# Fp32 state products on tiles of the PE array, weights kept in SBUF, and one string for every engine's order

## The chip, the cores and the metric

The kernel runs on one core of a Trainium2 chip. The metric is the device time of one execution in microseconds (us). Engines are named as the profile names them: PE is TensorE's matmul side and PEld its weight loads, DVE is VectorE, ACT is ScalarE, POOL is GpSimd, SP is the engine that issues all DMA transfers here.

## The reference

Eight batches b, eight heads h, 512 positions, 32 state rows, 64 numbers a head. Attention runs both ways between x and a small state, then the rows (512 of x and 32 of the state per batch) go through a two-layer network with softplus:

```python
scores = scale * np.matmul(x, state.transpose(0, 1, 3, 2))     # 512 x 32 per head
a = softmax(scores);   xread = np.matmul(a, state)
scores2 = scale * np.matmul(state, x.transpose(0, 1, 3, 2))    # 32 x 512 per head
a2 = softmax(scores2); sread = np.matmul(a2, x)
x = concat([xread, sread], axis=2) -> (8 * 544, 512)           # heads side by side
h = x @ w_in                                                   # 512 x 2048, float64 in memory
out = softplus(h) @ w_out                                      # 2048 x 512, float64 in memory
```

## The kernel before, in words

**Splitting.** The two layers run as fp32r matmuls. Each operand is split into a high part (a cast to fp32r, line 90, or line 83 on POOL) and a low part (the rest, line 91), and three products replace one (`PASSES`). The weights come as pairs of 32-bit words; `as_f32` (lines 102 to 116) makes fp32 of them with one ACT operation (line 111) and two of DVE (lines 114, 115).

**The state product.** The read `a @ state @ w_in` is associated the other way: for each batch V = state @ w_in is formed once per head, 256 x 2048 (32 state rows times 8 heads), and the first layer is a @ V (`gemm1`, line 475). So x's read is never formed. V of batches 0 to 3 comes from plain fp32 matmuls with a stationary matrix in which zeros pad each head (`QZ`; `make_v0`, lines 158 and 167, 256 columns each; `make_vf`, lines 200 and 211, 512 columns). Batches 0 and 1 stay in SBUF, 2 and 3 are written to DRAM (`Vd`). For batches 4 to 7 w_in, which was written to DRAM as fp32 (`wsc`), is read again, each head's 64 rows are split (`head`, lines 249 and 250) and multiplied with `StK` (`product`, line 235); the result goes to DRAM as well and is fetched by `fetch_v`. `split_v` makes the high and low part of a piece of 256 columns.

**Attention.** Per batch and half of the heads: scores (batches 0 and 1: plain fp32 with a zero-padded state, line 341; later: split x and split state, line 347), transposed 32 x 32 on DVE (355), maximum, subtraction, exp, sum, product, transposed back (371) and split; the state's side has exp (380), four PE transposes (392), the read of x (405 in plain fp32 for batches 0 and 1, 411 split) and a turn back (439 or 448).

**The layers.** A slot is one column tile of 128 of the hidden layer for one batch: six matmuls at line 475, softplus on ACT (462), the split, twelve matmuls at line 482 into four banks. 128 slots for x's rows and eight wider ones for the state's rows (`gemm1_read`, line 522), 136 softplus in all. Batches 0 and 1 take turns at first.

**Order.** Strings (`START`, `BLOCK`, `LAST`) give the order in which steps are written; the tile scheduler may then move instructions of an engine past one another. `MOVED` lists the operations that go to DVE or POOL instead of the usual engine. Of the eight PSUM banks two hold h, two everything of attention (`aux`) and four the second layer's sums.

Of the kernel before, what the change touches and what calls it, by code (L numbers as in the profile page):

```python
# [39 lines left out]
MOVED = {('R', 1, 0, 0, 0), ('R', 1, 0, 3, 0), ('R', 1, 0, 3, 1), ('R', 1, 1, 0, 0), ('R', 1, 1, 2, 0), ('R', 1, 1, 3, 1), ('R', 1, 2, 1, 0), ('R', 1, 3, 1, 0), ('at', 0, 1), ('at', 2, 1), ('at', 3, 0), ('g', 0, 13), ('g', 0, 5), ('g', 0, 6), ('g', 0, 7), ('g', 0, 8), ('g', 0, 9), ('g', 1, 1), ('g', 1, 10), ('g', 1, 11), ('g', 1, 12), ('g', 1, 14), ('g', 1, 7), ('g', 1, 8), ('g', 1, 9), ('g', 2, 2), ('g', 2, 5), ('g', 2, 6), ('g', 2, 7), ('g', 2, 8), ('g', 3, 6), ('g', 4, 10), ('g', 4, 11), ('g', 4, 7), ('g', 4, 8), ('hi', 'R', 1, 0, 1, 1), ('hi', 'R', 1, 0, 2, 1), ('hi', 'R', 1, 0, 3, 0), ('hi', 'R', 1, 0, 3, 1), ('hi', 'R', 1, 1, 3, 1), ('hi', 'R', 1, 2, 0, 1), ('hi', 'at', 1, 0), ('hi', 'at', 2, 0), ('hi', 'at', 3, 0), ('hi', 'g', 0, 13), ('hi', 'g', 0, 14), ('hi', 'g', 0, 5), ('hi', 'g', 0, 6), ('hi', 'g', 0, 9), ('hi', 'g', 1, 15), ('hi', 'g', 1, 7), ('hi', 'g', 1, 8), ('hi', 'g', 2, 1), ('hi', 'g', 2, 13), ('hi', 'g', 2, 15), ('hi', 'g', 2, 6), ('hi', 'g', 4, 12), ('hi', 'g', 4, 6), ('hi', 'g', 4, 8), ('hi', 'g', 4, 9), ('hi', 'g', 8, 2), ('hi', 'g', 8, 3), ('hi', 'g', 8, 4), ('hi', 'g', 8, 6), ('hi', 'v', 0, 1), ('hi', 'v', 0, 7), ('hi', 'v', 1, 1), ('hi', 'v', 1, 3), ('hi', 'v', 1, 5), ('hi', 'v', 1, 7), ('hi', 'v', 2, 2), ('hi', 'v', 2, 3), ('hi', 'v', 2, 5), ('hi', 'v', 2, 7), ('hi', 'v', 3, 1), ('hi', 'v', 4, 7), ('hi', 'wout', 0), ('hi', 'wout', 13), ('hi', 'wout', 14), ('hi', 'wout', 15), ('hi', 'wout', 7), ('hi', 'xh', 2, 0, 0), ('hi', 'xh', 2, 1, 0), ('hi', 'xs', 2, 0, 0), ('hi', 'xs', 2, 1, 1), ('hi', 'xs', 3, 1, 1), ('sr', 1, 0), ('tmul', 0, 0), ('tmul', 0, 1), ('tmul', 1, 1), ('tmul', 3, 0), ('tmul', 3, 1), ('tsub', 0, 0), ('v', 0, 0), ('v', 0, 3), ('v', 1, 0), ('v', 1, 4), ('v', 1, 5), ('v', 2, 3), ('v', 2, 7), ('v', 3, 0), ('v', 3, 2), ('v', 4, 7), ('v0', 0, 0, 1), ('v0', 0, 2, 2), ('v0', 1, 0, 2), ('v0', 1, 1, 1), ('v0', 1, 1, 2), ('v0', 1, 3, 2), ('vd', 3, 1, 0), ('vd', 3, 1, 1), ('vd', 3, 3, 0), ('ve', 0, 1, 5), ('ve', 0, 2, 1), ('ve', 0, 2, 3), ('ve', 0, 3, 1), ('ve', 0, 3, 7), ('ve', 1, 0, 1), ('ve', 1, 0, 2), ('ve', 1, 0, 3), ('ve', 1, 0, 6), ('ve', 1, 0, 7), ('ve', 1, 1, 0), ('ve', 1, 1, 1), ('ve', 1, 2, 5), ('ve', 1, 3, 4), ('wout', 0), ('wout', 15), ('xh', 2, 1, 0), ('xh', 2, 1, 1), ('xs', 2, 0, 1), ('xs', 2, 1, 0), ('xs', 3, 0, 1)}  # L40
# [5 lines left out]

@with_exitstack
def attention_then_softplus_mlp(ctx: ExitStack, tc, xn, xt, zq, zp, stk, w_in, w_out, out):
    nc = tc.nc
    nc.scalar.preload_act_table_set("natural_log_exp_and_others")  # L50
# [3 lines left out]
    dp = ctx.enter_context(tc.tile_pool(name="dp", bufs=1, space=DRAM))  # L54
    ps = ctx.enter_context(tc.tile_pool(name="ps", bufs=1, space=PSUM))
    uid = [0]

    def sb(tag, shape, dt=F32, bufs=1):
        uid[0] += 1
        return sp.tile(shape, dt, tag=tag, name=f"{tag}_{uid[0]}", bufs=bufs)  # L60

    def bank(tag, bufs):
        uid[0] += 1
        return ps.tile([P, 512], F32, tag=tag, name=f"{tag}_{uid[0]}", bufs=bufs)

    BANKS = {"aux": 2, "h": 2, "acc": 4}
    turn = cycle(("h", "acc", "acc"))
    early = [True]

    def aux():  # L70
        if early[0]:
            tag = next(turn)
            return bank(tag, BANKS[tag])
        return bank("aux", 2)

    ident = cp.tile([P, P], F32, name="ident")
    make_identity(nc, ident)

    def vec(*what):
        return nc.gpsimd if what in MOVED else nc.vector  # L80

    def pool_copy(dst, src):
        nc.gpsimd.tensor_scalar(dst, src, 1.0, 0.0, ALU.mult, ALU.add)  # L83


    def split(hi, lo, src, *what):
        if ("hi",) + what in MOVED:
            pool_copy(hi, src)
        else:
            nc.scalar.copy(hi, src)  # L90
        vec(*what).tensor_tensor(lo, src, f32(hi), ALU.subtract)  # L91

    def load_w(src, tag=None):
        w64 = src.dtype == I64
        tag = tag or ("k4" if w64 else "wt")
        t = sb(tag, src.shape, I64 if w64 else F32, bufs=K4 if tag == "k4" else 2)
        nc.sync.dma_start(t, src)
        return t
# [3 lines left out]


    def as_f32(t, tag="wt"):
        if t.dtype != I64:
            return t
        v = t.bitcast(I32).rearrange("p (n t) -> p n t", t=2)
        lo, hi = v[:, :, 0], v[:, :, 1]
        n = t.shape[1]
        h2 = sb("k2", [P, n], bufs=K2)  # L110
        nc.scalar.activation(h2, f32(hi), AF.Prelu, scale=2.0 ** -112, alpha=-(2.0 ** 32))  # L111
        r = sb(tag, [P, n], bufs=2 if tag == "wt" else 1)
        u = r.bitcast(I32)
        nc.vector.tensor_scalar(u, lo, 29, None, ALU.logical_shift_right)
        nc.vector.scalar_tensor_tensor(u, h2.bitcast(I32), 3, u, ALU.logical_shift_left, ALU.bitwise_or)  # L115
        return r

    wout = {}
    sreadT = cp.tile([P, 2, 4, B * NS], F32R, name="sreadT")
    Z4 = cp.tile([P, 4, P], F32, name="Z4")  # L120
    nc.gpsimd.memset(Z4, 0.0)

    ev = [0]

    def evac(dst, src):  # L130
        ev[0] += 1
        if ev[0] % 2:
            nc.vector.tensor_copy(dst, src)
        else:
            nc.scalar.copy(dst, src)  # L135

    wsc = [dp.tile([DM, 512], F32, tag=f"wsc{c}", name=f"wsc{c}") for c in range(4)]
    Vd = {}
    for c in range(4):
        Vd[0, c] = dp.tile([P, 4, 512], F32, tag=f"vd0_{c}", name=f"vd0_{c}")  # L140
        Vd[1, c] = dp.tile([H, P, 512], F32, tag=f"vd1_{c}", name=f"vd1_{c}")

    VTAGS = {1: ("wout10", "wout11"), 2: ("wout13", "wout14"), 3: ("vf", "vf")}
    QZ = [sb("QZ", [P, 4, P]), sb("wout15", [P, 4, P])]
    Vf, Vhl = {}, {}
    made = {}

    def make_v0():
        for b in range(2):
            Vf[b, 0] = sb("vf", [P, 2, 512], bufs=2)  # L150
        for half in range(2):
            cs = slice(256 * half, 256 * half + 256)
            for q in range(4):
                k = 4 * half + q
                wt = as_f32(first.pop(0), tag=f"wout{4 + k}" if k < 6 else "wt")
# [4 lines left out]
                for b in range(2):  # L160
                    dst, src = Vf[b, 0][r, q // 2, cs], pb[64 * b:64 * b + 64, 0:256]
                    if ("v0", half, q, b) in MOVED:
                        nc.vector.tensor_copy(dst, src)
                    else:
                        nc.scalar.copy(dst, src)
# [137 lines left out]
    def load_z(b):  # L303
# [9 lines left out]
        zin[b] = z  # L313

# [257 lines left out]

# [128 lines left out]
```

## Time and profile before

| | |
|---|---|
| three runs | 713.04, 713.7, 715.2 us; median 713.7 |
| span of the profiled execution | 709.8 us (its own time is not recorded beside it) |
| median less span | 3.9 us |
| PE, ACT, DVE, POOL busy | 96%, 60%, 54%, 24% of the span |
| first matmul of the first layer | at 32.70 us |
| HBM read and written | 56.62 MB, 25.69 MB |

The span runs from the first to the last instruction of the core. A matmul's record reaches from its start to its modelled end, so neighbours overlap: the gap between starts is what one costs in a full stream. A row of a group has the line, the engine, the operation, output and inputs, shapes, the count, then busy us and mean ns of one, then the idle time of the engine ahead of it with what ended that. Plain fp32 matmuls appear as two records each, fp32r ones as one.

### The profile page before, as it was taken

What the parts mean: (1) busy time and instruction counts of PE and PEld (TensorE: products, weight loads), DVE (VectorE), ACT (ScalarE), POOL (GpSimd) and SP (SyncE); (2) the same over time, 40 slices, a digit from 0 to 9 for tenths busy, and PEclk for the clock granted to TensorE, in tenths of its full rate; (3) what the DMA queues carried; (4) which work ended last, traced back from release to release, by engine and by line L of the source; (5) the groups of instructions that cost most, each with busy time, mean ns of one, the idle gap of its engine ahead of it and who ended that gap; (6) DMA issues with size and microseconds to landing.
All of it is one profiled execution on the core that took longest, in us unless ns stands there. A gap on an engine that the chain in (4) does not pass through costs nothing.

```text
span 709.8 us, 8853 instructions
## 1 busy us (share of the span) xinstructions
PE 678.6 (96%) x3012; PEld 534.1 (75%) x3012; DVE 384.2 (54%) x682; ACT 423.5 (60%) x701; POOL 172.9 (24%) x170
## 2 busy tenths in 40 slices
PE   5689899999999999999999999999999999999997
PEld 2455566888877778877788887888788888878886
DVE  4587547834696885595646633664376323432101
ACT  3699999935476575788658633863486334333222
POOL 1230102565333366111200070007000500100220
PEclk9999999999999999999999999999999999999999
DMA  8777767221244455364333321221012023412001
GB/s 273 267 261 259 262 212 242 98 60 40 80 141 148 149 166 186 116 193 155 120 104 108 101 59 31 97 83 30 30 53 67 22 70 90 149 30 60 1 0 59
DMA packets 42059, 82.87 MB, mean 117 GB/s; under 512 B 6176, under 2 KB 13088, under 8 KB 42016
## 3 DMA queue, kind: packets, MB, share of 16 engines
q1 hardware_dynamic: 42016, 82.33, 36.2%
q8 instruction: 23, 0.38, 0.2%
q14 instruction: 20, 0.16, 0.1%
HBM read 56.62 MB, written 25.69 MB: 116 GB/s over the span
## 4 chain that ended last, share of the span: by engine, by line
PE 75%; ACT 9%; DVE 7%; DMA 5%; issue 3%; SPq 1%; POOL 1%; DVEq 0%; ACTq 0%; POOLq 0%
PE acc L482 44%; PE h L475 20%; PE h L522 4%; DMA k<-in_w_in_dram 2%; PE aux L235 2%; ACT t L462 2%; PE aux L411 1%; DMA vf<-vd 1%; DVE glo L91 1%; PE aux L347 1%; DMA QZ<-in_zq_dram 1%; ACT k L111 1%; ACT ghi L90 1%; DMA vd<-ve 1%; PE aux L200 1%
## 5 line engine op out<-in xcount | busy, mean ns | idle before, releaser
L482 PE MATMUL acc<-wout,ghi 128*128 128x512 f32 x1088 | 344.2, 396 | 0.3 <-ACT o L135 0.3
L482 PEld LDWEIGHTS acc<-wout,ghi 128*128 128x128 f32 x1088 | 204.1, 189 | 47.9 <-issue 3.6
L482 PE MATMUL acc<-wout,glo 128*128 128x512 f32 x544 | 214.5, 394 | 0.0
L475 PE MATMUL h<-aT,vhl 128*128 128x512 f32 x768 | 200.6, 398 | 5.1 <-ACT t L462 3.7
L475 PEld LDWEIGHTS h<-aT,vhl 128*128 128x128 f32 x768 | 141.3, 188 | 43.9 <-ACT t L462 11.0
L91 DVE TENSOR_TENSOR glo<-t,ghi 128x512 fp32r<-128x512 f32 x100 | 71.9, 719 | 123.2 <-ACT ghi L90 65.0
L462 ACT ACTIVATE t<-h 128x512 f32<-128x512 f32 x136 | 81.1, 599 | 93.2 <-PE h L475 46.3
L482 PEld LDWEIGHTS acc<-wout,glo 128*128 128x128 f32 x544 | 102.4, 188 | 23.2 <-issue 1.2
L90 ACT CAST ghi<-t 128x512 fp32r<-128x512 f32 x104 | 64.6, 621 | 81.4 <-PE acc L482 80.6
L91 DVE TENSOR_TENSOR vhl<-vf,vhl 128x512 fp32r<-128x512 f32 x62 | 45.0, 726 | 89.2 <-ACT vhl L90 79.8
L83 POOL TENSOR_SCALAR ghi<-t 128x512 fp32r<-128x512 f32 x32 | 22.8, 712 | 175.3 <-PE acc L482 147.7
L91 POOL TENSOR_TENSOR glo<-t,ghi 128x512 fp32r<-128x512 f32 x36 | 49.0, 1362 | 46.0 <-ACT ghi L90 45.0
L90 ACT CAST vhl<-vf 128x512 fp32r<-128x512 f32 x59 | 36.5, 618 | 30.4 <-PE h L522 16.8
L368 POOL TENSOR_TENSOR T<-T,sm 128x512 f32<-128x512 f32 x13 | 13.7, 1052 | 136.7 <-DVE sm L367 136.2
L462 ACT ACT_TABLE_LOAD x30 | 38.5, 1283 | 3.9 <-PE h L475 3.4
L522 PEld LDWEIGHTS h<-sreadT,vhl 128*128 128x128 f32 x192 | 23.4, 191 | 4.4 <-ACT t L462 4.4
L522 PE MATMUL h<-sreadT,vhl 128*128 128x256 f32 x192 | 25.1, 287 | 1.1 <-ACT t L462 1.0
L352 DVE TENSOR_TENSOR k<-aux,k 64x512 f32<-64x512 f32 x24 | 16.4, 683 | 16.7 <-ACT k L351 16.4
L111 ACT ACTIVATE k<-k 128x512 f32<-128x512 f32 (+1 forms) x32 | 20.1, 642 | 8.6 <-DMA k<-in_w_in_dram 7.8
L115 DVE SCALAR_TENSOR_TENSOR wt<-k,wt 128x512 int32<-128x512 int32 (+1 forms) x26 | 20.0, 777 | 6.2 <-ACT k L111 5.8
L250 DVE TENSOR_TENSOR R<-wt,R 64x512 fp32r<-64x512 f32 x24 | 18.4, 768 | 6.9 <-ACT R L249 3.8
L235 PE MATMUL aux<-R,StK 128*128 128x512 f32 x64 | 20.0, 401 | 0.1
(162 smaller groups left out, 692.0 us busy)
## 6 DMA issues: line engine op xcount, KB each, us to landing
vd<-ve SPq DMA_DIRECT2D x44, 256.0 KB, 2.8
xT<-in_xt_dram SPq DMA_DIRECT2D x16, 512.0 KB, 4.1
x<-in_xn_dram SPq DMA_DIRECT2D x16, 512.0 KB, 3.9
k<-in_w_out_dram SPq DMA_DIRECT2D x16, 512.0 KB, 4.7
vf<-vd SPq DMA_DIRECT2D x64, 128.0 KB, 2.6
k<-in_w_in_dram SPq DMA_DIRECT2D x12, 512.0 KB, 5.4
out_dram<-o SPq DMA_DIRECT2D x24, 256.0 KB, 2.2
wt<-wsc SPq DMA_DIRECT2D x16, 256.0 KB, 2.9
```

The source lines that it names most:

```text
L83: nc.gpsimd.tensor_scalar(dst, src, 1.0, 0.0, ALU.mult, ALU.add)
L90: nc.scalar.copy(hi, src)
L91: vec(*what).tensor_tensor(lo, src, f32(hi), ALU.subtract)
L111: nc.scalar.activation(h2, f32(hi), AF.Prelu, scale=2.0 ** -112, alpha=-(2.0 ** 32))
L115: nc.vector.scalar_tensor_tensor(u, h2.bitcast(I32), 3, u, ALU.logical_shift_left, ALU.bitwise_or)
L235: nc.tensor.matmul(pb, StK[i][:, h, :], r, start=(i == 0), stop=(i == 1))
L250: vec("R", *what, o).tensor_tensor(r[z], wf[a], f32(r[a]), ALU.subtract)
L352: nc.vector.tensor_tensor(sc[64 * j:64 * j + 64], pb[0:64], s2, ALU.add)
L462: nc.scalar.activation(t, h, AF.Softplus)
L475: nc.tensor.matmul(h, Vhl[b, ft // 2][:, vi, g, cs], aT[b][:, ai, g], start=(n == 0), stop=(n == 5))
L482: nc.tensor.matmul(acc[c], g[gi][:, c0:c0 + P], wout[ft][:, wi], start=(ft == first and i == 0), stop=(ft == last and i == 2))
L522: nc.tensor.matmul(h[:, 256 * i:256 * i + 256], Whl[u, i][:, wi, kt, :], sreadT[:, si, kt, :], start=(n == 0), stop=(n == 11))
```

## The change

1. **Tiles.** `heads` multiplies, for one batch, the eight heads' states with w_in (or with x transposed): head 2q+e has its 64 numbers in partitions 64e to 64e+63, and its 32 state rows become output partitions 32q to 32q+31 of bank e. Each is one plain fp32 matmul of 64 x 32 with `tile_position=(64e, 32q)`. V for all batches (`v_product`, 33 calls: 31 of 512 columns, two of 256) and the scores of all batches (8 calls) are made in this way. The read of x (`s_read`, 16 calls) uses 128 x 32 tiles in plain fp32, four heads side by side, 64 columns each, 16 matmuls a call; the turn back (`s_back`) two 128 x 64 tiles.
2. **No scratch.** w_in is converted once and stays in SBUF as fp32 (`W`, 32 KB a partition); `wsc`, `Vd`, their writes and reads, `QZ`, `StK` and `z`'s split go. V is split straight out of the two banks, once per piece.
3. **Rooms.** SBUF tiles come from 27 rooms of 2 KB and 26 of 4 KB a partition (and five small ones), all eight PSUM banks from one list; a room is given out again in the order in which rooms were freed.
4. **Order.** A string of 1577 letters (`PLAN`) says which step is written next, `ENG` which engine takes each cast or element-wise step; `keep_in_program_order` holds each engine to that order, DMA issues on SP included.

The layers' matmuls, their shapes, the turns of batches 0 and 1 and the order of the slots are the same.

```diff
+class Ordered:
+    class Engine:
+        def __getattr__(self, name):
+            f = getattr(self.engine, name)
+            return lambda *a, **k: self.tc.keep_in_program_order(f(*a, **k))
...
+class Rooms:
+    def take(self, shape=None, dt=F32, uses=1):
+        tag = self.free.popleft()
...
+        t = self.pool.tile(shape or self.shape, dt, tag=tag, name=f"{tag}_{self.made}", bufs=1)
...
+    r2 = Rooms(sp, "s", N2, [P, 512])
+    r4 = Rooms(sp, "d", N4, [P, 2, 512])
+    banks = Rooms(ps, "b", 8, [P, 512])
...
+    ST = cp.tile([P, B, 4, 2 * NS], F32, name="ST")
+    W = cp.tile([P, 4, DFF], F32, name="W")
...
+    def heads(out_e, b, rhs):
+        for q in range(4):
+            for e in range(2):
+                r = slice(64 * e, 64 * e + 64)
+                nc.tensor.matmul(out_e[e][32 * q:32 * q + 32], ST[r, b, q, 32 * e:32 * e + 32], rhs(q)[r], start=True, stop=True,
+                                 tile_position=(64 * e, 32 * q))
+    def v_product():
+        for b, i in VLIST:
+            c0, c1 = units(b)[i]
+            t = Vb[b, i] = [banks.take(uses=2) for _ in range(2)]
+            heads([a[:, 0:c1 - c0] for a in t], b, lambda q: W[:, q, c0:c1])
...
+    def v_hi():
+                cast(t[0].t, Vb[b, i][e][:, 0:c1 - c0], engine())
+    def v_lo():
+                nc.vector.tensor_tensor(t[1].t, Vb[b, i][e][:, 0:c1 - c0], f32(t[0].t), ALU.subtract)
...
+    def scores():
+            heads(t, b, lambda q: xT[b, q // 2][:, q % 2])
...
+    def s_read():
+            for c in range(4):
+                for q in range(4):
+                    h = 2 * q + e
+                    nc.tensor.matmul(pr[k][32 * q:32 * q + 32, 0:D], a2T[k][:, P * c + 32 * q:P * c + 32 * q + 32],
+                                     x[b, h // 4][:, c, D * (h % 4):D * (h % 4) + D], start=(c == 0), stop=(c == 3),
+                                     tile_position=(0, 32 * q))
...
-    wsc = [dp.tile([DM, 512], F32, tag=f"wsc{c}", name=f"wsc{c}") for c in range(4)]
-                nc.tensor.matmul(pb, QZ[0][:, q, :], wf, start=True, stop=True)
-            nc.tensor.matmul(pb, StK[i][:, h, :], r, start=(i == 0), stop=(i == 1))
-        nc.sync.dma_start(Vd[1, c][h], ve)
...
+    run = {k: f() for k, f in steps.items()}
+    for k in PLAN:
+        now[0] = k
+        count[k] = count.get(k, 0) + 1
+        next(run[k])
```

PE around the first two first-layer matmuls, before: `aux`, `h` and `acc` are banks, `a2T` the state's weights turned, `vhl` split V. The rows at line 475 are the two.

```order
L405 MATMUL h_309<-x_206,a2T_307 128x256 x4
L341 MATMUL aux_316<-xT_257,Z_73 128x512 x2
L439 MATMUL h_344<-ident,sr_114 128x128 x4
L475 MATMUL h_357<-aT_113,vhl_297 128x512 x6
L475 MATMUL h_466<-aT_113,vhl_297 128x512 x6
L158 MATMUL acc_334<-wt_330,QZ_87 128x256
```

And now, where `b` are banks, `d` and `s` rooms, `v` small rooms, and every step carries line 84, that of `Ordered`:

```order
L84 MATMUL b_12_270<-ident,s_15_219 128x128 x4
L84 MATMUL b_13_291<-d_8_151,s_18_232 128x512 x2
L84 MATMUL b_13_291<-d_8_151,s_19_233 128x512
L84 MATMUL b_13_291<-d_13_217,s_20_253 128x512 x2
L84 MATMUL b_13_291<-d_13_217,s_21_254 128x512
```

Ahead of the first first-layer matmul now stand scores of two batches, one product of 256 columns and two reads, where before the twelve half-width products of `make_v0` and scores for three halves stood; the second product and its tiles follow behind it.

ACT in the stage where w_in and w_out are converted, around the third softplus before (`k` is a converted upper word, `t` a softplus, `wout` and `vf` copies of products or split weights):

```order
L462 ACT_TABLE_LOAD
L462 ACTIVATE t_515<-h_508 128x512
L207 COPY wout_105_389<-aux_433 64x512
L207 COPY wout_106_390<-aux_433 64x512
L90 CAST wout_142_498<-wt_501 128x512
L90 CAST ghi_517<-t_515 128x512
L111 ACT_TABLE_LOAD
L111 ACTIVATE k_151_523<-k_140_493 128x512
```

And now around the fifth softplus (rooms `s` written from `b` are softplus, those written from `d` converted upper words):

```order
L84 ACT_TABLE_LOAD
L84 ACTIVATE s_46_452<-d_17_275 128x512
L84 ACTIVATE s_51_483<-d_16_266 128x512
L84 ACTIVATE s_53_490<-d_19_285 128x512
L84 ACTIVATE s_55_495<-d_18_278 128x512
L84 ACTIVATE s_59_523<-d_20_317 128x512
L84 ACT_TABLE_LOAD
L84 ACTIVATE s_60_532<-b_29_516 128x512
L84 ACT_TABLE_LOAD
L84 ACTIVATE s_61_534<-d_21_333 128x512
```

The copies of products (line 207) are gone from ACT, the casts of the split are mostly on other engines here, and five conversions stand together ahead of the fifth softplus.

More of the change, by code (lines that the diff above doesn't have):

```diff
@@ L1 @@
+from collections import deque
 from contextlib import ExitStack
-from itertools import cycle
 import concourse.bass as bass
@@ L58, in sb @@
[L58 to L74, printed above, removed]
@@ L76, in attention_then_softplus_mlp @@
-    ident = cp.tile([P, P], F32, name="ident")
[L77 to L98, printed above, removed]
@@ L104, in as_f32 @@
[L104 to L116, printed above, removed]
@@ L454, in split_wout @@
-    def split_wout(ft):
-        assert ft < NFT - 1 or all(made[0, c] == 3 for c in range(1, 4))
-        wout[ft] = sb(f"wout{ft}", [P, 2, DM], F32R)
-        w = as_f32(ahead("out"))
-        split(wout[ft][:, 0], wout[ft][:, 1], w, "wout", ft)
-    def softplus(h, *what):
-        t = sb("t", [P, 512], bufs=2)
-        nc.scalar.activation(t, h, AF.Softplus)
-        ghi = sb("ghi", [P, 512], F32R, bufs=3)
-        glo = sb("glo", [P, 512], F32R, bufs=3)
-        split(ghi, glo, t, "g", *what)
-        return ghi, glo
@@ L485, in store @@
-    def store(acc, dsts, tags="oooo"):
-        for a, d, tag in zip(acc, dsts, tags):
-            o = sb(tag, [P, DM], F32, bufs=2)
-            evac(o, a)
-            if len(d.shape) == 2:
-                nc.sync.dma_start(d, o)
-            else:
-                for i in range(4):
-                    nc.sync.dma_start(d[i], o[32 * i:32 * i + 32])
-    def chain(*gens):
-        for f in gens:
-            yield from f()
-    wv = [w.rearrange("(g j o d) f -> j d g o f", g=2, j=2, o=2) for w in wsc]
@@ new lines, in place, with shaped, win_upper, win_lower @@
+    def place(k):
+        q, n, c0, c1 = PIECES[k]
+        return W[:, q:q + n, c0:c1]
+    def shaped(t, k):
+        n = PIECES[k][1]
+        return t.rearrange("p (n f) -> p n f", n=n) if n > 1 else t.unsqueeze(1)
+    up, low = {}, {}
+    def win_upper():
+        for k in range(len(PIECES)):
+            t = up["i", k] = r2.take()
+            upper(t.t, win[k].t)
+            win[k].done()
+            yield
+    def win_lower():
+        for k in range(len(PIECES)):
+            t = low["i", k] = r2.take()
+            lower(t.t, win[k].t)
+            win[k].done()
+            yield
@@ new lines, in win_join, with wout_upper, wout_lower @@
+    def win_join():
+        for k in range(len(PIECES)):
+            u, l = up["i", k], low["i", k]
+            join(place(k), shaped(u.t, k), shaped(l.t, k))
+            u.done()
+            l.done()
+            yield
+    wf, wout = {}, {}
+    def wout_upper():
+        for k in range(NFT):
+            t = wf[k] = r2.take(uses=2)
+            upper(t.t, wraw[k].t)
+            wraw[k].done()
+            yield
+    def wout_lower():
+        for k in range(NFT):
+            t = low["o", k] = r2.take()
+            lower(t.t, wraw[k].t)
+            wraw[k].done()
+            yield
@@ new lines, in wout_join, with wout_hi, wout_lo @@
+    def wout_join():
+        for k in range(NFT):
+            l = low["o", k]
+            join(wf[k].t, wf[k].t, l.t)
+            l.done()
+            yield
+    def wout_hi():
+        for k in range(NFT):
+            wout[k] = r4.take([P, 2, DM], F32R)
+            cast(wout[k][:, 0], wf[k].t, engine())
+            wf[k].done()
+            yield
+    def wout_lo():
+        for k in range(NFT):
+            elementwise(wout[k][:, 1], wf[k].t, f32(wout[k][:, 0]), ALU.subtract, engine())
+            wf[k].done()
+            yield
@@ new lines, in s_read @@
+    def s_read():
+        for k in PAIRS:
+            b, e = k
+            pr[k] = banks.take()
+            for c in range(4):
+                for q in range(4):
[3 more added lines that the diff above has]
+                                     tile_position=(0, 32 * q))
+            a2T[k].done()
+            x[b, 0].done()
+            x[b, 1].done()
+            yield
@@ new lines, in s_scale, with s_back @@
+    def s_scale():
+        for k in PAIRS:
+            sr[k] = r1.take()
+            if engine() == "D":
+                nc.vector.tensor_scalar_mul(sr[k].t, pr[k][:, 0:D], rs[k])
+            else:
+                nc.scalar.activation(sr[k].t, pr[k][:, 0:D], AF.Copy, scale=rs[k])
+            pr[k].done()
+            few[k].done()
+            yield
+    srt = {}
+    def s_back():
+        for b in range(B):
+            srt[b] = banks.take(uses=2)
+            for e in range(2):
+                r = slice(64 * e, 64 * e + 64)
+                nc.tensor.matmul(srt[b][r, 0:P], sr[b, e].t, ident, start=True, stop=True, tile_position=(0, 64 * e))
+                sr[b, e].done()
+            yield
@@ new lines, in softplus, with g_hi, g_lo @@
+    def softplus():
+        for k in SLOTS:
+            tt[k] = r2.take(uses=2)
+            nc.scalar.activation(tt[k].t, hb[k].t, AF.Softplus)
+            hb[k].done()
+            yield
+    def g_hi():
+        for k in SLOTS:
+            ghi[k] = r2.take(dt=F32R, uses=2)
+            cast(ghi[k].t, tt[k].t, engine())
+            tt[k].done()
+            yield
+    def g_lo():
+        for k in SLOTS:
+            glo[k] = r2.take(dt=F32R, uses=2)
+            elementwise(glo[k].t, tt[k].t, f32(ghi[k].t), ALU.subtract, engine())
+            tt[k].done()
+            yield
@@ new lines, in attention_then_softplus_mlp, with gemm2 @@
+    acc = {}
+    ends = []
+    def gemm2():
+        for b, ft in SLOTS:
+            first, last = next(r for r in RUNS.get(b, [(0, NFT // 2 if b == B else NFT)]) if r[0] <= ft < r[1])
+            last -= 1
+            g = (ghi[b, ft], glo[b, ft])
+            for half in range(2):
+                for i in range(2):
+                    c = i if b == B else 2 * half + i
+                    if ft == first and (b < B or half == 0):
+                        acc[b, c] = banks.take()
+                    f = 2 * ft + half if b == B else ft
+                    c0 = 256 * half + P * i if b == B else P * c
+                    lead = ft == first and (b < B or half == 0)
+                    tail = ft == last and (b < B or half == 1)
+                    for n, (gi, wi) in enumerate(PASSES):
+                        nc.tensor.matmul(acc[b, c].t, g[gi][:, c0:c0 + P], wout[f][:, wi],
+                                         start=(lead and n == 0), stop=(tail and n == 2))
+                    if tail:
+                        ends.append((b, c, first, last, acc[b, c]))
+                for v in g:
+                    v.done()
+                yield
@@ new lines, in attention_then_softplus_mlp, with evacuate @@
+    parts, stores = {}, []
+    def evacuate():
+        while True:
+            b, c, first, last, a = ends.pop(0)
+            final = b == B or last == NFT - 1
+            if b == B or (b, c // 2) not in parts:
+                o = r2.take() if final else None
+                if not final:
+                    if c % 2 == 0 and (b, c // 2, "new") not in parts:
+                        parts[b, c // 2, "new"] = r4.take(uses=2)
+                    o = parts[b, c // 2, "new"]
+                    dst = o[:, c % 2]
+                    if c % 2 == 1:
+                        parts[b, c // 2] = o
+                else:
+                    dst = o.t
+                cast(dst, a.t, engine())
+            else:
+                o = parts[b, c // 2]
+                dst = o[:, c % 2]
+                nc.vector.tensor_tensor(dst, a.t, dst, ALU.add)
+            a.done()
+            if final:
+                stores.append((b, c, dst, o))
+            yield
@@ new lines, in store @@
+    def store():
+        state = out.rearrange("(b r) m -> b r m", r=ROWS)[:, S:, :]
+        while True:
+            b, c, src, o = stores.pop(0)
+            if b == B:
+                for i in range(4):
+                    nc.sync.dma_start(state[4 * c + i], src[32 * i:32 * i + 32])
+            else:
+                nc.sync.dma_start(out[b * ROWS + P * c:b * ROWS + P * c + P], src)
+            o.done()
+            yield
+    steps = {
+        "S": load_state, "T": load_xT, "X": load_x, "I": load_win, "O": load_wout,
+        "a": win_upper, "b": win_lower, "c": win_join,
+        "A": wout_upper, "B": wout_lower, "C": wout_join, "D": wout_hi, "E": wout_lo,
+        "v": v_product, "h": v_hi, "l": v_lo,
+        "Q": scores, "1": a_turn, "2": a_max, "3": a_sub, "4": a_exp, "5": a_sum, "6": a_mul, "7": a_back,
+        "8": a_hi, "9": a_lo, "e": s_max, "f": s_exp, "i": s_sum, "t": s_turn, "u": s_copy, "R": s_read,
+        "r": s_scale, "y": s_back, "z": s_hi, "Z": s_lo,
+        "w": w_hi, "x": w_lo, "g": gemm1, "s": softplus, "m": g_hi, "n": g_lo, "G": gemm2,
+        "o": evacuate, "p": store,
+    }
```

735 lines of the change are left out of this document (286 added, 449 removed).

## The prediction

> **What bounds the kernel now.** I read the page's head first, then the stages, then the chain of waits, and last PE's timeline for the price of one matmul of each kind. The page:
>
> ```profile
> span 709.8 us, 8853 instructions
> PE 678.6 (96%) x3012; PEld 534.1 (75%) x3012; DVE 384.2 (54%) x682; ACT 423.5 (60%) x701; POOL 172.9 (24%) x170
> PE 75%; ACT 9%; DVE 7%; DMA 5%; issue 3%; SPq 1%; POOL 1%; DVEq 0%; ACTq 0%; POOLq 0%
> ```
>
> PE is busy 96% and carries 75% of the chain that ended last. The other engines have room on average, so the stages must say where they do not. The windows, cut at the first first-layer matmul (32.7), at 108 and at the end; the columns are each engine's busy time, granted clock, DMA share and GB/s:
>
> ```profile
> 0.00:32.70 32.70, 19.20 (x64) 11.10 (x65) 14.80 (x40) 14.44 (x33) 6.96 (x12) 1.00 0.78 257
> 36.00:108.00 72.00, 64.39 (x230) 41.80 (x229) 47.80 (x94) 69.71 (x112) 9.25 (x9) 0.98 0.75 247
> 108.00:150.00 42.00, 41.36 (x173) 31.57 (x172) 29.78 (x40) 34.93 (x54) 21.21 (x18) 1.00 0.46 155
> 150.00:650.00 500.00, 495.72 (x2299) 402.45 (x2298) 278.82 (x489) 286.79 (x474) 125.02 (x121) 1.00 0.30 94
> ```
>
> Three regimes. Up to 32.7 us DMA feeds everything and PE is idle two fifths of the time. From 36 to 108 us ScalarE is busy 69.71 of 72 us and PE is idle 7.6. From 108 on PE has hardly a gap: there only fewer PE microseconds help. So I price PE's work by what it streams, from gaps between starts (a record's own length includes its way through the array). A stretch of the chain, then starts in PE's timeline:
>
> ```profile
> 404.98 8.24 PE acc L482 x36
> ```
>
> ```profile
> 59.40 1.98 PE L341 MATMUL aux<-xT,Z 128*128 128x512 f32 x4
> 61.22 1.02 PE L200 MATMUL aux<-wt,QZ 128*128 128x512 f32 x2
> ...
> 100.24 1.02 PE L200 MATMUL aux<-wout,QZ 128*128 128x512 f32 x2
> 101.10 1.02 PE L211 MATMUL aux<-wout,wout 128*128 128x512 f32 x2
> ```
>
> A split (fp32r) matmul of 512 columns costs 8.24/36 = 0.229 us. Of plain fp32, one matmul is two records: from 100.24 to 101.10 one product passes, 0.86 us, 0.43 a record, four times nearly the fp32r price (59.40 to 61.22 gives 0.91 for the same thing in a gappier place). I scale by columns. The counts, by line (count, then busy us and mean ns; a mean of 396 against a gap of 229 also says that emptying the array costs about 0.17 us):
>
> ```profile
> L482 PE MATMUL acc<-wout,ghi 128*128 128x512 f32 x1088 | 344.2, 396 | 0.3 <-ACT o L135 0.3
> L482 PE MATMUL acc<-wout,glo 128*128 128x512 f32 x544 | 214.5, 394 | 0.0
> L475 PE MATMUL h<-aT,vhl 128*128 128x512 f32 x768 | 200.6, 398 | 5.1 <-ACT t L462 3.7 <-ACT aT L90 1.1
> L522 PE MATMUL h<-sreadT,vhl 128*128 128x256 f32 x192 | 25.1, 287 | 1.1 <-ACT t L462 1.0
> L235 PE MATMUL aux<-R,StK 128*128 128x512 f32 x64 | 20.0, 401 | 0.1
> L411 PE MATMUL aux<-k,a2T 128*128 128x256 f32 x96 | 13.6, 284 | 0.8 <-DVE a2T L91 0.8
> L347 PE MATMUL aux<-k,zhl 128*128 128x512 f32 x48 | 13.0, 389 | 0.0
> L341 PE MATMUL aux<-xT,Z 128*128 128x512 f32 x16 | 9.7, 735 | 6.4 <-DMA Z<-in_zp_dram 5.0 <-DMA xT<-in_xt_dram 1.4
> ```
>
> The two layers: 2400 x 0.229 = 549.6 and 192 x 0.115 = 22.1, together 571.7. Attention and state products: L235 14.7, L347 11.0, L411 11.0, L341 16 x 0.43 = 6.9; the code gives 24 products at L200 and L211 (48 records, 20.6), 16 half-width ones at L158 and L167 (6.9), 16 at L405 (6.9), and 84 transposes of 128 columns at 0.1 (8.4). Sum 86.4. PE streams 658.1 of 709.8; 51.7 us are not streamed.
>
> **The change, part by part.** *Two layers.* Same matmuls, same shapes, same order of slots: 571.7 stays.
>
> *State products and scores.* L158, L167, L200, L211, L235, L341, L347 go, 60.1 us. In their place stand 31 products of 512 and two of 256 columns, and eight sets of scores: 40 full ones, each of eight fp32 matmuls on eight disjoint tiles of 64 rows by 32 columns. Before has no tile at all, so the price x of one is bounded: all eight abreast is one pass of 512 columns as at L200, 0.86; one after another is 8 x 0.86 = 6.9. I take the row at the lower end, because the eight write disjoint partitions or banks, have no semaphore between them and together fill the cells that one L200 product fills; with one emptying x = 1.1, so 44. [...]
>
> *Read of x.* L405 and L411 go (17.9). Sixteen reads come, each of 16 fp32 matmuls of 64 columns, 32 records of 0.43/8 = 0.054: from 0.43 (four column tiles abreast) to 1.7, with 0.17 of emptying 0.6 to 1.9. I take 1.1: 17.6. Transposes: 64 x 0.108 = 6.9, and the eight turns back 3.5. PE then streams 571.7 + 44 + 17.6 + 6.9 + 3.5 = 643.7, 14.4 less.
>
> *Start.* The rows:
>
> ```profile
> 4.99 3.75 PE L341 MATMUL aux<-xT,Z 128*128 128x512 f32 x4 [4.99 <-DMA Z<-in_zp_dram]
> ...
> 32.70 1.64 PE L475 MATMUL h<-aT,vhl 128*128 128x512 f32 x6
> ```
>
> Afterwards scores need both halves of x transposed and the state, 1.2 MB: at 257 GB/s about 7 us. Then VectorE's order up to the first first-layer matmul holds, by the durations of
>
> ```profile
> L355 DVE STREAM_TRANSPOSE T<-k 128x512 f32<-128x512 f32 x12 | 8.5, 705 | 0.1
> L359 DVE TENSOR_REDUCE mx<-T 128x16 f32<-128x512 f32 x16 | 10.8, 678 | 0.0
> L115 DVE SCALAR_TENSOR_TENSOR wt<-k,wt 128x512 int32<-128x512 int32 x24 | 19.3, 807 | 6.2 <-ACT k L111 5.8
> L114 DVE TENSOR_SCALAR wt<-k 128x512 int32<-128x512 int32 x24 | 12.0, 507 | 2.1 <-PE aux L211 1.1 <-DMA k<-in_w_in_dram 0.7 <-DMA wsc<-wt 0.2
> ```
>
> six transposes (4.2), ten large reductions (6.8), four shifts (2.0), two joins (1.6) and 3.7 of small ones: 18.3 us, so about 26. The weights do not end later: 3.9 MB stand ahead of the second piece of w_in, 17 us, plus some 4 of conversion. The first first-layer matmul moves from 32.7 to 26. Of PE's work 15.1 lay before it (36 records of fp32 at 512 or 256 columns, two reads, transposes), afterwards 6.7.
>
> *ScalarE, VectorE, scratch.* ScalarE falls from 687 rows to 400. Ahead of and with the first twelve softplus stand ten table loads, 38 wide and six narrow operations:
>
> ```profile
> L462 ACT ACTIVATE t<-h 128x512 f32<-128x512 f32 x136 | 81.1, 599 | 93.2 <-PE h L475 46.3 <-DVE glo L91 36.9 <-POOL glo L91 8.6
> L462 ACT ACT_TABLE_LOAD x30 | 38.5, 1283 | 3.9 <-PE h L475 3.4
> L111 ACT ACTIVATE k<-k 128x512 f32<-128x512 f32 x28 | 18.4, 671 | 1.0 <-DMA k<-in_w_out_dram 0.7 <-DMA k<-in_w_in_dram 0.2
> ```
>
> 10 x 1.28 + 12 x 0.60 + 38 x 0.64 + 6 x 0.3 = 46 us, while PE comes to the twelfth first-layer matmul at about 26 + 34 = 60. ScalarE is no longer last there; PE and then the weights' transfers are (by ScalarE's order, five conversions stand ahead of the fifth softplus; 9.7 MB are loaded by then, 38 us, against PE at 36). The scratch in DRAM goes at no price: after 108 us DMA is a third busy and its cover, PE, stays; before 108 it is what shortens the queue. Not streamed after the first first-layer matmul are now 709.8 - 32.7 - 643.0 = 34.1 us, some 4 of them the last store. I let 7.6 of visible and about as much of hidden waiting go with the ScalarE stage and keep 19; the bounds are 34 (all of it only moves) and 8.
>
> *Pinned order and shared rooms.* No row of before prices them. Each engine now stands at its head until that instruction can run: behind a softplus that waits for a first-layer matmul stand ScalarE's casts of V and of the state, behind these PE's next first-layer matmul; behind a load that waits for its room on SP stand all later loads and stores. A V product holds two of the eight banks until two casts and two subtractions have read them (0.62 and 0.72 us each), where before a copy freed its bank. What this could give back is already in the 19; what it could cost has its own rival.
>
> **The sum.** 26 + (643.7 - 6.7) + 19 = 682 us of span. The times shown have a median of 713.7, 3.9 over the profiled span; the profiled execution's own time stands nowhere else. With the same 3.9: 686.
>
> **Rivals.** *Two abreast only.* Each tile's fp32 matmul is two records, and this part of the weight loads' timeline (100.67 and on) shows one load and one record every 0.43, the load one deep:
>
> ```profile
> 100.67 0.19 PEld L211 LDWEIGHTS aux<-wout,wout 128*128 128x128 f32 x1 [0.24 <-issue]
> 101.10 0.19 PEld L211 LDWEIGHTS aux<-wout,wout 128*128 128x128 f32 x1 [0.24 <-issue]
> 101.53 0.19 PEld L482 LDWEIGHTS acc<-wout,ghi 128*128 128x128 f32 x1 [0.24 <-issue]
> ```
>
> If PE starts records strictly in order, a tile's second record must wait for its first, and all tiles behind it wait too: only the second of one and the first of the next overlap. Then x = 8 x 0.43 = 3.4, with emptying 3.6, 100 us more: 786, slower. It decides from x = 1.8 on, where the gain of 28 is spent. [...] Against it: no row of before has two records on different cells of the array, so nothing shows that the second may not pass the first's wait. Chance 0.19.
>
> *Half the overlap.* Only one direction of tiles runs abreast, x = 1.9: 32 us more, 718. Chance 0.1. *The fixed order stalls.* An instruction at an engine's head that is late by 0.25 us in each of 136 slots gives 34 us: 720. For it, the softplus waits of 46.3 and 36.9 above that a free order now fills with other work; against it, PE's queue holds most of a slot of work by then. Chance 0.08. *No overlap at all*, the change not doing what it says: x = 6.9, 232 more, 918. Chance 0.03.
>
> **The numbers.** The forecast has 0.6; its own range is 664 (x at 0.9 and reads at 0.6 give 8 each, waits at 13 give 6) to 706 (waits at 34 cost 15, reads at 1.4 cost 5). The range takes in the cases at 718 and 720 with 15 above them, and leaves out those at 786 and 918, 0.22 together: 664 to 735. A difference under 0.3%, about 2 us, cannot be told from no change in these measurements. Faster: 0.57 of the forecast, 0.05 from the good ends of the cases at 718 and 720: 0.62. Same 0.03, from where these cross 713.7. Slower 0.35: 0.22 from the two tall cases, 0.12 from the two middle ones, 0.01 from the forecast.
>
> **What would show it.** Starts of the eight tile matmuls of one product: if they lie within a few hundredths, and the next matmul on the whole array comes 1.0 to 1.2 us after the first, x holds; steps of 0.43 are the rival. First first-layer matmul near 26; ScalarE under 85% between 36 and 108; PE idle by record below 10 us from there to the end, else the order stalls. A product over 1.8 us makes the prediction wrong whatever the rest does.

## The result, and the profile after

| | before | after |
|---|---|---|
| median of four runs | 714.45 us | 673.44 us |
| span of the profiled execution | 709.8 us | 671.6 us |
| first matmul of the first layer | 32.70 us | 29.18 us |
| ACT, DVE busy | 423.5, 384.2 us | 272.3, 305.0 us |
| HBM read, written | 56.62, 25.69 MB | 34.60, 8.91 MB |

The ratio is 0.9413, with an interval from 0.9378 to 0.9448: 41 us less. The forecast was 686 in a range from 664 to 735. The two spans differ by 38.2 us, not 41: the profiled execution before was a quick one (spans of the same kernel in the later runs lie from 710.0 to 717.7). The head, the slices of PE, its clock and DMA, and the chain of the changed kernel's page:

```profile
span 671.6 us, 9540 instructions
PE 647.7 (96%) x3856; PEld 498.0 (74%) x3856; DVE 305.0 (45%) x543; ACT 272.3 (41%) x414; POOL 190.6 (28%) x181
PE   4698999999999999999999999999999999999997
PEclk9698999999999999999999999999999999999999
DMA  8991321200340210301040004000010000101002
PE 91%; DVE 6%; DMA 1%; issue 1%; ACT 0%; SPq 0%; DVEq 0%; ACTq 0%
```

PE is 96% busy as before, of a shorter span. Its share of the chain rose from 75% to 91%: ScalarE, 9% of the chain before, is out of it, and what is left beside PE is VectorE. DMA is at eight to nine tenths for three slices of 17 us and at four or less from then on, where before it was at six to eight tenths for seven slices of 18. The stages, cut where those of before were cut (columns as there):

```profile
0.00:32.70 32.70, 17.54 (x144) 7.88 (x144) 21.15 (x46) 14.12 (x28) 12.15 (x16) 0.79 0.95 353
36.00:108.00 72.00, 68.64 (x344) 50.67 (x344) 57.47 (x95) 50.46 (x67) 28.52 (x25) 0.98 0.42 150
108.00:150.00 42.00, 42.00 (x271) 33.00 (x270) 32.09 (x53) 29.82 (x42) 13.64 (x12) 1.00 0.12 39
```

From 36 to 108 us ScalarE fell from 69.71 to 50.46 busy and PE's idle time from 7.6 to 3.4. The clock of 0.79 in the first stage is new.

PE's timeline has the first first-layer matmul (29.18), the price of a product (128.98 to 130.00), of a transpose group (131.49 to 131.84), of two products in a row (159.28 to 161.16), of a turn back (411.33 to 411.70) and of the layers (403.76 to 411.33 for 33):

```profile
29.18 3.27 PE L84 MATMUL b<-d,s 128*128 128x512 f32 x12
...
128.98 1.09 PE L84 MATMUL b<-W,ST 64*32 64x512 f32 x16
130.00 1.65 PE L84 MATMUL b<-d,s 128*128 128x512 f32 x6
131.49 0.60 PE L84 MATMUL b<-ident,s 128*128 128x128 f32 x4
131.84 1.63 PE L84 MATMUL b<-d,s 128*128 128x512 f32 x6
...
159.28 1.95 PE L84 MATMUL b<-W,ST 64*32 64x512 f32 x32
161.16 5.73 PE L84 MATMUL b<-d,s 128*128 128x512 f32 x24
...
403.76 7.64 PE L84 MATMUL b<-d,s 128*128 128x512 f32 x33
411.33 0.44 PE L84 MATMUL b<-ident,v 128*64 128x128 f32 x4
411.70 1.09 PE L84 MATMUL b<-W,ST 64*32 64x512 f32 x16
```

Eight matmuls of plain fp32, 16 records, pass in 1.02 us, or 0.94 each for two products in a row. Before, one such matmul on the whole array took 0.86.

### The profile page after: what moved, and what is told of

Read it like the earlier page. It is cut to its first block, busy times and chain, and to the rows that moved or that the text cites. A ratio compares the mean times of both kernels' runs of the same rounds, so it can differ in the third digit from the quotient of the medians.

```text
span 671.6 us, 9540 instructions
## 1 busy us (share of the span) xinstructions
PE 647.7 (96%) x3856; PEld 498.0 (74%) x3856; DVE 305.0 (45%) x543; ACT 272.3 (41%) x414; POOL 190.6 (28%) x181
## 3 DMA queue, kind: packets, MB, share of 16 engines
q1 hardware_dynamic: 15808, 43.52, 18.8%
HBM read 34.60 MB, written 8.91 MB: 65 GB/s over the span
## 4 chain that ended last, share of the span: by engine, by line
PE 91%; DVE 6%; DMA 1%; issue 1%; ACT 0%; SPq 0%; DVEq 0%; ACTq 0%
PE b L84 91%; DVE s L84 4%; DVE v L84 1%; DMA d<-in_xt_dram 1%; DVE W L84 1%; ACT L84 0%; DVE d L84 0%; ACT s L84 0%; SPq L84 0%; DVE sreadT L84 0%; DVEq L84 0%; ACTq L84 0%
## 5 line engine op out<-in xcount | busy, mean ns | idle before, releaser
L84 PE MATMUL b<-d,s 128*128 128x512 f32 (+1 forms) x2912 | 570.8, 364 | 2.2 <-ACT s L84 1.1
L84 PEld LDWEIGHTS b<-d,s 128*128 128x128 f32 (+1 forms) x2912 | 455.7, 176 | 121.5 <-issue 19.0
L84 ACT ACTIVATE s<-b 128x512 f32<-128x512 f32 x136 | 80.0, 598 | 236.2 <-PE b L84 223.2
L84 POOL TENSOR_TENSOR s<-s,s 128x512 fp32r<-128x512 f32 x69 | 93.1, 1352 | 247.4 <-PE b L84 104.8
L84 DVE TENSOR_TENSOR s<-s,s 128x512 fp32r<-128x512 f32 x67 | 53.5, 813 | 57.6 <-PE b L84 39.0
L84 POOL TENSOR_SCALAR s<-s 128x512 fp32r<-128x512 f32 x45 | 30.4, 682 | 108.7 <-ACT s L84 65.6
L84 DVE TENSOR_TENSOR s<-b,s 128x512 fp32r<-128x512 f32 (+1 forms) x66 | 43.1, 665 | 36.5 <-ACT s L84 36.1
L84 DVE CAST s<-s 128x512 fp32r<-128x512 f32 x49 | 26.6, 545 | 62.9 <-ACT s L84 35.3
L84 PE MATMUL b<-W,ST 64*32 64x512 f32 (+1 forms) x528 | 37.2, 596 | 8.7 <-DVE W L84 8.1
L84 POOL TENSOR_TENSOR d<-s,d 128x512 fp32r<-128x512 f32 x20 | 28.1, 1403 | 22.7 <-ACT d L84 11.3
```

The costliest lines, as they stand in the source:

```text
L84: return lambda *a, **k: self.tc.keep_in_program_order(f(*a, **k))
```

## What the experiments showed

All times are medians; what is said to be more or less is against 673.44 of the changed kernel unless another is named. Each ratio to the kernel before, run beside it, has its 95% interval.

### Half of the tiles: no_row_tiles

```diff
-  nc.tensor.matmul(out_e[e][32*q:32*q+32], ST[r, b, q, 32*e:32*e+32], rhs(q)[r], ..., tile_position=(64*e, 32*q))
+  nc.tensor.matmul(out_e[e][32*q:32*q+32], ST[:, b, q, 32*e:32*e+32], rhs(q), ..., tile_position=(0, 32*q))
```

> The changed kernel, with every product and score made by matmuls of 128 rows (the other head's rows of the state are zeros) on four column tiles, so two matmuls follow one another on each tile. Result unchanged. Theory A (the eight tiles run abreast, and PE's streamed work sets the time after the start): a full product goes from 1.02 us to about 1.9, 40 x 0.87 = 35 us more, 708 us. Rival B (PE has slack for this, or the time comes from less ScalarE and DMA work alone): within 8 us of 673.

702.93 us, ratio 0.984 [0.9811, 0.9869]: 29.5 more. Its timeline:

```profile
135.00 1.94 PE L84 MATMUL b<-W,ST 128*32 128x512 f32 x16
136.88 0.50 PE L84 MATMUL b<-d,s 128*128 128x512 f32 x1
```

A product takes 1.88 us, 0.86 more, and 40 x 0.86 = 34. Theory A holds and B falls: PE has no slack for it, save 5 us. This run's trace shows where some 3.4 of them are. Scores and products ahead of the first first-layer matmul, 2.5 full ones, cost 2.1 us more, but that matmul starts only 1.2 later (30.38). PE's wait for VectorE's join of w_in is 1.23 us (at 59.16) and not the 2.05 of the changed kernel (at 55.84), and the 3.4 us at half clock behind it, 1.7 us of work, do not come.

### Each product twice: twice, twice_adjacent

```diff
-        for q in range(4):
+        for q in [0, 1, 2, 3] * 2:          # twice
             for e in range(2):
...
+                for _ in range(2):          # twice_adjacent, in place of the line above
                     nc.tensor.matmul(out_e[e][32*q:32*q+32], ...)
```

> The changed kernel, with each product and each set of scores computed twice into the same banks. Theory A: 40 x 0.94 = 38 us more, 711 us, no matter where the product stands. Rival B (PE has slack): under 15 us more.

705.61 us, 0.9864 [0.9836, 0.9892]: 32.2 more, less than the 38 because the second of two products in a row costs 0.86 and not 0.94 (136.33 to 138.21 for both), which makes 34, and because the first first-layer matmul comes only 0.9 later (30.04), though 2.1 us of the additional work lie ahead of it:

```profile
136.33 1.95 PE L84 MATMUL b<-W,ST 64*32 64x512 f32 x32
138.21 0.50 PE L84 MATMUL b<-d,s 128*128 128x512 f32 x1
```

> The changed kernel, with each tile's matmul of products and scores issued twice in a row on its own tile (four records next to each other on one tile), where the run with whole products repeated had two and then fourteen on other tiles. Theory A1 (a tile takes one running record and one with its weights loaded, and a third one blocks all that stand behind it): every tile holds the next one up for two records, 8 x 2 x 0.43 + 0.86 = 7.7 us a product, 40 x 6.7 = 270 us more, near 940. Theory A2 (each tile has a queue of its own): the same as the run with whole products repeated, 706. Rival B of strict program order: at least as slow as A1.

707.7 us, 0.9882 [0.9848, 0.9917]. Four records in a row on one tile cost what two and two did:

```profile
132.62 1.99 PE L84 MATMUL b<-W,ST 64*32 64x512 f32 x32
134.54 0.73 PE L84 MATMUL b<-d,s 128*128 128x512 f32 x2
```

1.92 us for the pair. A1, and with it strict program order, would have shown 7.7. The eight tiles' first records start 13 ns apart, each tile's second 0.45 us after its first: when the next tile starts, three of the tile's four records have not.

### The read of x, tile by tile: read_by_tile

```diff
-            for c in range(4):
-                for q in range(4):
+            for q in range(4):
+                for c in range(4):
```

> The changed kernel, with the two loops of the read of x exchanged: the four matmuls of one column tile now stand next to each other (q outside, c inside) where before neighbours were on different tiles. If matmuls of different tiles can start only in program order, a read goes from 0.48 us to 32 x 0.054 = 1.7 and the kernel gets 20 us longer, 693. If a tile's queue lets the next tile's matmul past, nothing changes: 673.

683.95 us, 0.9565 [0.9542, 0.9588]: 10.5 more, half of what strict order would cost and not nothing, so both forms of the expectation were off. The reads' group, first in the changed kernel, then in this one:

```profile
L84 PE MATMUL b<-d,s 128*32 128x64 f32 x512 | 10.7, 233 | 0.0
```

```profile
L84 PE MATMUL b<-d,s 128*32 128x64 f32 x512 | 22.2, 228 | 0.0
```

11.5 us more busy for the sixteen reads, 0.72 a read. The single starts in the trace say how. A record does not name its tile; which is whose is read off the lengths (four records of 243 ns, taken as the first of each tile, the others 219) and the steps of 0.056 between one tile's records. Of one read in this run, in us:

```
tile 0   244.568 .648 .704 .760 .816        then its last three
tile 1                                 244.821
```

Tile 1 starts only when five of tile 0's eight records have started and three wait; tiles 2 and 3 come in the same way, at 245.075 and 245.328. In the run above three waited on each tile as well, there from the tile's first record on, and the next tile started 13 ns later. With eight records in a row on one tile the next tile starts 0.253 us later here, and a read takes some 1.31 us (0.59 and the 0.72). What sets this is not shown.

### The order set free: unpinned

```diff
-PIN = True
+PIN = False
```

> The changed kernel, with the scheduler free to move instructions of an engine past one another (the string then only sets the order in which steps are written). Theory A (after the start PE's work sets the time): within 8 us of 673 either way. Rival C (the fixed order is what keeps the waits at 19 us): 15 to 40 us longer.

674.02 us, 0.9419 [0.9394, 0.9445]: the same. The scheduler did move work (in its run two reads stand ahead of the first state product, and the first first-layer matmul starts at 26.31 instead of 29.18), and lost it again by waits such as that at 36.36, behind which the granted clock is at half from 37.07 to 40.49:

```profile
26.31 3.23 PE L539 MATMUL b<-d,s 128*128 128x512 f32 x12
29.47 0.44 PE L477 MATMUL b<-ident,v 128*64 128x128 f32 x4
29.84 0.65 PE L451 MATMUL b<-d,s 128*32 128x64 f32 x32
30.43 0.64 PE L299 MATMUL b<-W,ST 64*32 64x256 f32 x8
...
36.36 4.04 PE L539 MATMUL b<-d,s 128*128 128x512 f32 x10 [2.04 <-DVE s L323]
```

Rival C falls: holding the engines to the string neither made the gain nor cost any. What another string would cost was not tried. The same rows give a read's price, 29.84 to 30.43: 0.59.

### Both halves of the overlap undone: half_overlap

The edits of no_row_tiles and read_by_tile together.

> The changed kernel with both undone at once: products on four column tiles of 128 rows, and the read of x tile by tile. Result unchanged. If PE's streamed work is the whole of it, the two losses add: 673.4 + 29.5 + 10.5 = 713, the time of the kernel before. If they are hidden by one another: 703.

711.97 us, 0.9949 [0.9925, 0.9973]: 38.5 more, nearly the 40 of the two apart. With half the overlap of its tiles the changed kernel, with its start, its string and without scratch, is 0.5% faster than the one before. By the sum its other parts gain some 20 us, which products at 1.88 and reads at 1.31 spend again.

### The kernel before without its scratch: before_no_scratch

```diff
-                nc.sync.dma_start(wsc[c][P * q:P * q + P, :], wf)
-        nc.sync.dma_start(Vd[1, c][h], ve)
...
-                nc.sync.dma_start(wf, wsc[c][P * q:P * q + P, :])
+                nc.sync.dma_start(wf, xt[c, :, q, :])
```

> The kernel before, without any write of w_in or of V to DRAM; what was read back from there is read from x in memory instead, in pieces of the same shape, so V of batches 2 to 7 and the state rows are computed from other numbers, by the same instructions. 44 plus 20 writes fewer and no wait for them. Theory A (ScalarE ends the stage from 36 to 108 us, PE all after): at most 8 us less, 706 to 714. Rival D (DMA is what holds the early stage, so that dropping the scratch is a main part of the gain): 15 us less or more, under 700.

707.47 us against 714.93, 0.9875 [0.9841, 0.991]: 7.5 less, at the edge of theory A. The two traces show only half of it (spans of 706.0 and 709.8), as the profiled execution before was a quick one. V of batches 2 to 7 is not the state's in this kernel, since it leaves out what the scratch carried; the instructions are the same. The stage from 36 to 108 us in that run:

```profile
36.00:108.00 72.00, 66.64 (x245) 43.10 (x244) 45.49 (x88) 70.86 (x112) 7.25 (x8) 1.00 0.49 169
```

DMA's share falls from 0.75 to 0.49 and PE gets 2.3 us more of the stage, but ScalarE stays at 98%: with DMA half idle it is ScalarE that fills the stage. What freeing ScalarE alone would give was not tried.

### VectorE in the early stage: early_dve, casts_only, warm

```diff
-    'h': "AAADADAA...   'z': "ADAAADDA"   'D': "ADPAPP...   'm': "PPPDDD...
+    'h': "AAAAAAAA...   'z': "AAAAADDA"   'D': "AAPAPP...   'm': "PPPADD...
...
-            nc.vector.tensor_scalar_add(sm[k], sm[k], EPS)     # early_dve and warm only
-            nc.vector.tensor_scalar_add(rs[k], rs[k], EPS)     # early_dve and warm only
...
+            for _ in range(22 if (b, i) == VLIST[0] else 0):   # warm only
+                nc.tensor.matmul(t[0][:, 0:P], ident, ident, start=True, stop=True)
```

> The changed kernel, with five casts of the first 55 us moved from VectorE to ScalarE and without the addition of 1e-9 to the softmax sums (they are at least 1, so fp32 does not change). About 3.1 us less for VectorE before 56 us. Theory E (VectorE, busy without a gap from 10.6 to 56 us, ends the early stage of the changed kernel): 2 to 3 us less, 671. If DMA or PE's clock ends it: 673 to 675.

668.15 us, 0.9328 [0.9299, 0.9357]: 5.3 less, the shortest median here together with warm's. The windows around 57 us, of the changed kernel and then of this one, say why it is more than the 3.1 us of work that were taken away:

```profile
50.00:57.00 7.00, 4.95 (x43) 2.55 (x43) 6.54 (x9) 2.10 (x5) 4.37 (x4) 1.00 0.44 145
57.00:61.00 4.00, 4.00 (x12) 2.20 (x9) 1.64 (x4) 3.97 (x7) 0.01 (x1) 0.57 0.00 0
```

```profile
50.00:57.00 7.00, 6.91 (x50) 3.65 (x49) 4.89 (x9) 5.66 (x11) 4.33 (x4) 1.00 0.24 94
57.00:61.00 4.00, 4.00 (x19) 3.30 (x19) 4.00 (x8) 2.57 (x5) 1.29 (x1) 1.00 0.00 0
```

In the changed kernel PE has 2.05 us of idle time at 55.84, for VectorE's join of the last rows of w_in's columns 512 to 1023, and the granted clock then drops to half for 3.4 us, 1.7 us of work lost. Both are gone here. The rest is the first first-layer matmul at 27.92, 1.3 earlier. The wait in the changed kernel, with the join that ends it and an earlier one:

```profile
51.46 0.68 DVE L84 SCALAR_TENSOR_TENSOR W<-s,s 128x512 int32<-128x512 int32 x1
...
54.02 1.77 DVE L84 SCALAR_TENSOR_TENSOR W<-s,s 128x512 int32<-128x512 int32 x1
```

```profile
55.84 2.52 PE L84 MATMUL b<-W,ST 64*32 64x512 f32 x20 [2.05 <-DVE W L84]
```

The join that PE waits for takes 1.77 us, the earlier one of the same shape 0.68. POOL is idle at 51.46 and makes a subtraction from 53.98 to 55.24. Eleven more of VectorE's instructions before 57 us are 0.2 to 1.1 us longer than quick ones of their kind in this run, some 9 us with this one, and each of them runs beside one of POOL's. So VectorE's stage may be as long as it is through POOL's work too; moving POOL's work away was not tried.

> The changed kernel with only the five early casts moved from VectorE to ScalarE; the additions of 1e-9 stay. VectorE has about 1.8 us less to do before 56 us. Theory E (VectorE ends the early stage): half or more of the 5.3 us, as soon as PE's wait at 55.8 us goes and with it the 3.4 us at half clock behind it: 669 to 671. If the shorter chain of the sums made the gain: 673.

669.43 us, 0.9367 [0.934, 0.9393]: 4.0 less; no half clock at 57 us either. The five casts are the larger part. That the shorter chain of sums gives the last 1.3 is not shown by the medians, as the runs of each version differ by more than 2 among themselves. The traces show 1.0 of it. Counted from the scores that wait for x's second half, the first first-layer matmul comes 20.58 us later here and in the changed kernel (8.60 to 29.18), and 19.59 in early_dve; the rest is when that half landed. Early_dve, then casts_only:

```profile
8.33 3.96 PE L84 MATMUL b<-d,ST 64*32 64x512 f32 x24 [0.50 <-DMA d<-in_xt_dram]
...
27.92 2.99 PE L84 MATMUL b<-d,s 128*128 128x512 f32 x12
```

```profile
9.08 4.24 PE L84 MATMUL b<-d,ST 64*32 64x512 f32 x24 [1.14 <-DMA d<-in_xt_dram]
...
29.66 3.02 PE L84 MATMUL b<-d,s 128*128 128x512 f32 x12
```

> The version with less early work for VectorE, and 22 matmuls of the identity with itself on PE ahead of the first state product, where PE waits for the first columns of w_in; their bank is overwritten by the product. If PE then stays at full clock from 17 to 27 us, the reads and transposes there take about 2 us less: the first first-layer matmul near 26.5, 666. If VectorE alone sets that stage: 668, no change; if the matmuls come too late and hold the product up: 669 or more.

668.17 us, 0.9349 [0.9324, 0.9375]: no change against 668.15. The first product comes at 21.78 instead of 21.96, the first first-layer matmul at 27.68 instead of 27.92, which counted as above is 19.54 us and no gain:

```profile
15.80 5.08 PE L84 MATMUL b<-ident 128*128 128x128 f32 x44
21.78 0.64 PE L84 MATMUL b<-W,ST 64*32 64x256 f32 x8 [0.91 <-DVE W L84]
23.46 0.96 PE L84 MATMUL b<-W,ST 64*32 64x256 f32 x8 [1.04 <-DVE W L84]
```

With the filling the clock was full until 23.6 (half from there to 27.1, where early_dve has half from 17.0 to 27.2), and PE waited for VectorE's joins just the same. That stage is VectorE's.

## Why the prediction was right, point by point

**The sum.** After the first first-layer matmul PE streams the products at 40 x 0.98 = 39 (44 forecast), the reads at 16 x 0.59 = 9.4 (17.6), transposes at 64 x 0.088 = 5.6 (6.9), turns at 8 x 0.37 = 3.0 (3.5); with the layers' 571.7 that is 628.7 instead of 643.7, of which 5.1 lie ahead. 671.6 - 29.2 - 623.6 leaves 18.8 not streamed. So the forecast's 26 + 637.0 + 19 was 29.2 + 623.6 + 18.8. The mechanism held, and two errors, of 13 and 3 us, partly cancel; the term most wrong is the read of x, too dear by 8, then the products, by 5. In the other direction the start was 3 too early. What lies around the span was 2.3 us in the profiled execution, not 3.9; in the runs of the kernel before that list both, it is 1.7 to 2.7 as well, so the 3.9 set a quick execution's span against the median of others.

**Tiles.** The step on which all hung, x at the lower end of 0.86 to 6.9, was right: 1.02 by itself. The rival of two abreast, at 3.6, is refuted by the starts: of the product at 128.98, eight records start within 46 ns (128.978 to 129.024), the other eight from 129.431 to 129.478. Strict program order, on which that rival rests, is not what these runs show: with each tile's matmuls next to each other in the program (twice_adjacent), the eight tiles still started 13 ns apart and each tile's second record 0.45 us after its first. Eight passes of 0.86 one after another, the other end, would be 6.7 times the 1.02.

**The read.** I had bounded it by 0.6 and 1.9 and taken 1.1, near the middle, with no row for it. Sixteen matmuls go through at the lower bound, 0.59, with a loop that changes tile at each step. read_by_tile, some 1.31 a read, shows that this is a matter of the order in the code.

**The start.** VectorE's sum was good (18.3 forecast; from its first transposition at 10.58 to the end of the subtraction at 28.1, 17.6), its beginning was not: x's second half landed at 8.56 and the scores ended after 10, where I had 7. Six loads were issued by 3.1 us and landed one after another, the last at 11.77.

**ScalarE's stage.** Forecast under 85%, it is 70%. PE is last there, as forecast, but behind it come not the transfers: up to 56 us what PE waits for is VectorE, which has no gap over half a microsecond from 10.6 on. The 7.6 visible and as much hidden that I let go came out right in sum (34.1 to 18.8). That it fits so closely is partly luck: the new wait and the half clock behind it, 3.8 us together, are inside the 18.8, and nothing in the forecast stood for them. PE's idle time by record from the first first-layer matmul to the end fell from 17.7 to 8.8 us, under the 10 named.

**Order, rooms, scratch.** The rival of a stalling order had no effect (unpinned). The rooms were not tried by themselves. The scratch had no price of its own in the forecast; taken out of the kernel before it gives 7.5 us, in the traces hardly any of it after 108 us (PE 0.7 us busier there), as forecast, so it lies in the stages that the 19 was meant to cover.

**Where 38.2 us of span went.** 19.4 are PE's work after the first first-layer matmul (643.0 to 623.6), 15.3 time not streamed (8.9 of it idle by record), 3.5 the start. The experiments show that the first part hangs on the overlap of the tiles: half of it undone costs 38.5. How the waits divide between ScalarE's relief and the scratch is shown only as far as 7.5 us for the scratch in the kernel before; ScalarE's relief was not tried by itself.

## What to carry to other kernels

Small plain fp32 matmuls on disjoint tiles of the PE array overlapped almost fully here, both records of each (1.02 us for eight against 0.86 for one whole-array matmul). Two in a row on one tile were no harm (1.92 us for two products in twice_adjacent, 1.88 in twice), four in a row were (0.72 more a read in read_by_tile): put the loop over tiles inside. Then a split into high and low parts seems not worth its casts for heads of 64 by 32: before, line 235 made sixteen such products (four batches, four pieces of 512 columns) in 14.7 us by the price of its matmuls, 0.92 each, against 0.98 now without a cast. That is a sum and was not tried. When one engine's stage is relieved, sum up the others' instructions up to the next matmul: the next bound stood there in this kernel, and behind a wait of 2.05 us for it 3.4 us at half clock cost another 1.7.

## What the hardware did that was not expected

With four records in a row on each tile (twice_adjacent) the tiles started 13 ns apart, with eight in a row (read_by_tile) 0.253 us apart, in both with three records of the tile before still waiting. The clock was granted at half from 16.0 to 29.7 us in the changed kernel, though PE was in work for half of it with transposes, products of 256 and reads of 64 columns (the row of that window, with PE's busy time and then the granted clock of 0.51); with 44 whole-array records of 128 columns ahead (warm) it was full until 23.6:

```profile
16.00:30.00 14.00, 7.40 (x95) 4.52 (x94) 13.25 (x30) 7.64 (x17) 8.53 (x8) 0.51 1.03 405
```

Behind three of PE's idle times came 3.4 us at half clock: 2.16 us up to 39.52 in the kernel before (half from 40.15 to 43.56), 2.05 up to 55.84 in the changed kernel (57.00 to 60.41) and 2.04 up to 36.36 in unpinned (37.07 to 40.49). Behind 1.77 us up to 76.04 in the kernel before and 1.23 up to 59.16 in no_row_tiles came none. That the idle time alone is the cause is not shown.

And DMA moved more in the changed kernel's first 32.7 us than in that of before, 353 against 257 GB/s, with no scratch and larger loads; dropping the scratch alone left it at 258, so the cause is elsewhere and was not tried.
